# Layer 1's first-matmul weights of the first half: split ahead, kept in DRAM as fp16 pairs, read back in place

## The chip, the cores and the metric

The kernel runs on one core of a Trainium2 chip. The core has a matrix engine (TensorE, PE), a vector engine (VectorE, DVE), a scalar engine (ScalarE, ACT), a general engine (GpSimd, POOL) and a sync engine (SP), which here only issues DMAs; ACT and POOL issue DMAs too. Each engine works through its own list of instructions in order and waits on semaphores for the others. 16 DMA engines move data between DRAM (HBM) and the on-chip memory SBUF (128 partitions). The metric is the device time of one execution in microseconds (us), the median of several runs.

## What is computed

A gated scan over 10112 tokens of 256 numbers (two sequences of 5056), and after it two mixture-of-experts layers with 8 experts, each token going to one expert. Cut to what matters:

```
h = f[:, t] * h + (1 - f[:, t]) * x[:, t];  y[:, t] = h          # scan, f from f_logit and lower_bound
# layer 0 and layer 1 (other routers, the same shape)
expert_idx = argmax(logits, axis=1);  gate_w = max of softmax(logits)
for e in range(8):
    mask = expert_idx == e
    out[mask] = gate_w[mask, None] * (relu(x[mask] @ w1[e]) @ w2[e])   # w1[e] 256x1024, w2[e] 1024x256
```

All inputs and outputs are float32. The kernel keeps precision with fp16 pairs: a number times 64 is written as hi (rounded to fp16) plus lo (the remainder, fp16), and products of hi and lo parts are added up.

## The kernel before, in words

Tokens are sorted by expert into tables in DRAM (X[0] for layer 0, X[1] for layer 1), in tiles of 128 rows of one expert each. The hidden width of 1024 is cut into two halves of 512, h = 0 and h = 1. One **unit** is one tile with one half: `mm1` multiplies the transposed tile xT with the half's W1 (24 matmuls into a PSUM tile hps, line L801), `evac` makes the fp16 pair hT from it (ACT writes hi, L809, DVE writes lo), and three units later `mm2` multiplies hT with the half's W2 (L821, L824, into ops).

A host loop over **slots** writes the order of the whole program: slot i holds `mm1` and `evac` of unit i, `mm2` of unit i - 3 (`LAG`), and everything that `at(slot, priority, function, ...)` has put there, by priority. On PE, ACT, POOL and SP this written order is the order in which the engine works from slot 17 on; DVE's order is set by the framework's scheduler. There are 332 units: 166 of layer 0, then 166 of layer 1.

The weights of one half, all 8 experts, fill W1[h] and W2[h] in SBUF, and there is room for two halves. So around the change of layer the order of units is different (the **swap**): the last 21 tiles of layer 0 go through half 0 first (units 124 to 144) and then through half 1 (units 145 to 165). Once unit 144 is done, W1[0] and W2[0] are free, and during units 145 to 165 layer 1's half 0 is put there. Layer 1 begins with 21 tiles of half 0 (units 166 to 186), during which layer 1's half 1 is put in place.

A weight of one expert and half comes as 128 x 1024 float32 (512 KB) and is put in place in steps written by `wstep`: `w_load` brings it to a buffer ws (three buffers; a DMA that ACT issues, L371); two steps later `w_hi` writes hi with ACT (L384); three steps later `w_lo` writes lo with DVE (a SCALAR_TENSOR_TENSOR; most of DVE's work is recorded under helper lines, L183 for this form). `wplan(items, start, step)` puts 16 such items (8 of W1, 8 of W2) into slots `start + k * step`. For layer 1's half 0 these are slots 148 on, 0.98 slots apart.

Beside this, SP issues one transposing DMA per tile that brings xT from the table X (L770, four buffers, so that the one for unit u waits until unit u - 4 has read its buffer), and in layer 0 a small DMA exr (L783). After a tile's second half its result goes through the routing of layer 1: a chain over ACT, DVE, PE (x2p L910, logits lp L928, ranks RK) and POOL, which scatters the finished row trow into X[1] (L988). At slot 121 an If on all engines covers the last tiles of layer 0. The scan and the routing of layer 0 run beside the first units and end around slot 105; `checkpoint` then makes the last table of tiles, and POOL writes padding rows (L676) behind the tokens of each expert.

DMAs of SP and ACT signal their end on eight semaphores, DMAHW0 to DMAHW7, in turn (DMASW for POOL's); a DMA that gets a semaphore waits until the DMA that had it before has landed.

Of the kernel before, what the change touches and what calls it, by code (L numbers as in the profile page):

```python
# [10 lines left out]
F16 = mybir.dt.float16  # L11
I32 = mybir.dt.int32
U32 = mybir.dt.uint32
ACTF = mybir.ActivationFunctionType
ALU = mybir.AluOpType
AX = mybir.AxisListType

P = 128
D = 256
E = 8  # L20
F = 1024
HF = 512
# [39 lines left out]
 'sc': (0, 26),  # L62
 'exg': 'SSS',
 'w1': (-8, 0.8),
 'w2': (0, 0.75),
 'w3': (0, 0.9),
 'wprio': 60,
 'p': {'load': (-2, 2),
# [54 lines left out]
def scan_moe_moe_kernel(ctx, tc, xf, emb, cst, tmp, w1a, w2a, w1b, w2b, out, seq, cfg=CFG):  # L123
# [11 lines left out]
    LAG = cfg["lag"]  # L135
# [26 lines left out]
    qp = Pool(ctx.enter_context(tc.tile_pool(name="qp", bufs=6)))  # L162
# [7 lines left out]
    dr = ctx.enter_context(tc.tile_pool(name="dr", bufs=1, space=bass.MemoryType.DRAM))  # L170
# [2 lines left out]
    pr = ctx.enter_context(tc.tile_pool(name="pr", bufs=1, space=bass.MemoryType.PSUM))  # L173

    X = [dr.tile([DUM + P, RW // 2], I32, name=f"X{m}") for m in range(2)]
    W1 = [wp.tile([P, E, 2, 2, HF], F16, name=f"W1_{h}") for h in range(2)]
    W2 = [wp.tile([P, E, 4, 2, D], F16, name=f"W2_{h}") for h in range(2)]

    V, A, G, T, SP = nc.vector, nc.scalar, nc.gpsimd, nc.tensor, nc.sync

    def stt(eng, out, in0, s, in1, op0, op1, **kw):
        assert eng is V
        return eng.scalar_tensor_tensor(out=out, in0=in0, scalar=s, in1=in1, op0=op0, op1=op1, **kw)  # L183
# [180 lines left out]
    def w_load(item):  # L364
        m, which, h, e = item
        k = 8 * which + e
        if (m, h) == (0, 0) and k < 8 + cfg["wal"]:
            t = W1[1][:, k % 8].rearrange("p k b f -> p (k b f)").bitcast(F32)
        else:
            t = st.tile([P, 1024], F32, name="ws", tag="ws")  # L370
        hwq().dma_start(out=t, in_=wsrc[m][which][:, h, e, :])  # L371
        return t
# [13 lines left out]
    def w_lo(item, t):  # L386
        src, hi, lo = w_parts(item, t)
        m, which, h, e = item
        k = cfg["wg"][2 * m + h]
        i = 8 * which + e  # L390
        on_g = k and (i * k) // 16 != ((i + 1) * k) // 16
        if on_g:
            ts(G, src, src, 64.0, None, ALU.mult)
            tt(G, lo, src, hi, ALU.subtract)
        else:
            stt(V, lo, src, 64.0, hi, ALU.mult, ALU.subtract)

    def w_sub(item, t):

# [619 lines left out]
    for m in range(2):  # L1019
# [14 lines left out]
        for part in (tl, tails[m]):  # L1034
            for j in range(0, len(part), CT):
                d = dict(t=part[j:j + CT], at=j)
# [25 lines left out]
    def at(s, prio, fn, *a):  # L1062
        seqn[0] += 1
        slots.setdefault(s, []).append((prio, seqn[0], fn, a))
# [10 lines left out]
    for c in range(NCH):  # L1075
        b = s0[c]
# [9 lines left out]
        if c % 2 or c == NCH - 1:  # L1086
            q = c // 2
# [3 lines left out]
            b, prio = s0[c] + PO["put"][0], PO["put"][1]  # L1091
# [14 lines left out]
    def wseq(m, h):  # L1106
        return [(m, 0, h, e) for e in range(E)] + [(m, 1, h, e) for e in range(E)]

    wdone = set()
    wbuf = {}  # L1110
# [26 lines left out]
    def wplan(items, start, step, ahead=0):  # L1137
        x = start

        def it(k):  # L1140
            return items[k] if 0 <= k < len(items) else None

        if ahead:
            for k in range(len(items)):
                at(max(first - 2, int(start + (k - ahead) * step)), cfg["wlp"], wstep, it(k), None, None, None)
        for k in range(len(items) + 4):
            at(int(x), cfg["wprio"], wstep, None if ahead else it(k), it(k - 2), it(k - 3), it(k - 4))
            x += step

    last_h0 = [i for i, u in enumerate(units) if u[0]["m"] == 0 and u[1] == 0][-1]  # L1150
# [1 line left out]
    at(last0 + cfg["t0at"][0], cfg["t0at"][1], lambda: last_tiles(0))  # L1152
    wplan(wseq(0, 0), first + 1, cfg["wstep0"], cfg["wa"])
    wplan(wseq(0, 1), *cfg["w1"])
    wplan(wseq(1, 0), last_h0 + 1 + LAG + cfg["w2"][0], cfg["w2"][1] * cfg["swap"] / 16.0)
    wplan(wseq(1, 1), n1 + LAG + cfg["w3"][0], cfg["w3"][1] * cfg["swap"] / 16.0)

    loaded = [0]
# [232 lines left out]
```

## Time and profile before

| | |
|---|---|
| median of 3 runs | 1102.36 us (1089.52, 1102.36, 1105.03) |
| the profiled execution | 1096.34 us, span from first to last instruction 1094.5 us |
| mean granted clock of TensorE | 0.968 of full speed |
| PE busy | 983.7 us, 90% of the span |
| DVE busy | 684.3 us, 63% |
| ACT busy | 522.0 us, 48% |
| POOL busy | 505.1 us, 46% |
| moved by DMA | 124.12 MB, 113 GB/s over the span |

Shares over the span are averages over stages with different limits: the scan with layer 0's beginning, layer 0, the swap, layer 1. They are read stage by stage, with the waits and the rows of each. L-numbers are lines of the kernel; a line can be that of a helper, so groups are told apart by the tiles that they write and read (`W<-ws` is the split of a weight). SPq and ACTq are DMA issues on those engines' queues.

### The profile page before, as it was taken

The page shows a single profiled execution, that of the slowest core. Times are in us where ns is not written, and L with a number is a line of the kernel's source. Part 1 is how long each engine was busy: PE and PEld are TensorE (multiplying, and loading weights), DVE is VectorE, ACT ScalarE, POOL GpSimd, SP SyncE. Part 2 cuts the span into 40 slices and gives each one's busy share as a digit, 9 for nine tenths or more (in the row PEclk, how much of TensorE's full clock was granted, in tenths as well). Part 3 has the DMA queues.
Part 4 walks back from the last instruction along what each step waited for, and adds up shares of the span by engine and source line. Part 5 has one row for each costly group of instructions (what it writes and reads, how often), then busy time and mean ns, then how long its engine had stood idle before and what let it go on. Part 6 is the DMA issues. An engine that isn't in the chain of part 4 may idle for free.

```text
span 1094.5 us, 33440 instructions
## 1 busy us (share of the span) xinstructions
PE 983.7 (90%) x11935; PEld 795.2 (73%) x11935; DVE 684.3 (63%) x2116; ACT 522.0 (48%) x1298; POOL 505.1 (46%) x1009
## 2 busy tenths in 40 slices
PE   2532889999999999989999789999999999999996
PEld 2322668888888888867877678788788788788885
DVE  7867777888788777744649988866333333333332
ACT  5645556565656655444337655633333333333332
POOL 4888576667666666722103676145222222222222
PEclk9965999999999999998999999999999999999999
DMA  9448935676577765332339749943222322222120
GB/s 366 183 147 246 189 89 113 114 147 135 123 138 134 139 121 106 99 60 51 66 73 209 174 107 221 215 99 94 52 53 50 50 54 52 48 50 44 45 53 26
DMA packets 191620, 124.12 MB, mean 113 GB/s; under 512 B 169329, under 2 KB 170110, under 8 KB 191456
## 3 DMA queue, kind: packets, MB, share of 16 engines
q1 hardware_dynamic: 167344, 48.97, 24.7%
q10 hardware_dynamic: 11488, 39.33, 13.8%
q0 software_dynamic: 12624, 33.62, 11.2%
q8 instruction: 104, 1.70, 0.7%
q14 instruction: 60, 0.49, 0.2%
HBM read 54.70 MB, written 34.66 MB: 82 GB/s over the span
## 4 chain that ended last, share of the span: by engine, by line
PE 43%; DVE 5%; DMA 3%; issue 1%; POOL 1%; ACT 0%; POOLq 0%; DVEq 0%; ACTq 0%
PE hps L801 21%; PE ops L821 14%; PE ops L824 7%; DMA X<-trow,tsl 2%; DVE W L183 2%; DMA ws<-w2b 1%; DVE hT L183 1%; DMA ws<-w1b 1%; DVE trow L183 1%; DVE osum L191 1%; DVE trow L187 0%; POOL X L988 0%; DVE tsc L188 0%; POOL ob L191 0%; DVE tse L188 0%
## 5 line engine op out<-in xcount | busy, mean ns | idle before, releaser
L801 PE MATMUL hps<-xT,W 128*128 128x128 f16 x7968 | 506.4, 220 | 12.9 <-DMA xT<-X 10.0
L801 PEld LDWEIGHTS <-W 128*128 x7968 | 476.2, 98 | 53.8 <-issue 10.4
L821 PE MATMUL ops<-W,hT 128*128 x1328 | 452.6, 381 | 15.6 <-DVE hT L183 7.4
L183 DVE SCALAR_TENSOR_TENSOR hT<-hps,hT 128x512 f16<-128x512 f32 x332 | 228.2, 687 | 238.5 <-ACT hT L809 238.3
L824 PE MATMUL ops<-W,hT 128*128 x1328 | 363.5, 274 | 0.0
L809 ACT ACTIVATE hT<-hps 128x512 f16<-128x512 f32 x332 | 198.0, 597 | 300.0 <-PE hps L801 288.9
L821 PEld LDWEIGHTS <-hT 128*128 128x128 f16 x1328 | 130.1, 98 | 130.9 <-DVE hT L183 7.7
L1008 POOL DMA_INDIRECT out<-osum,ti x83 | 81.1, 977 | 290.4 <-DVE osum L183 259.0
L824 PEld LDWEIGHTS <-hT 128*128 128x128 f16 x1328 | 130.2, 98 | 18.5 <-issue 6.0
L988 POOL DMA_INDIRECT X<-trow,tsl x83 | 89.0, 1073 | 56.0 <-DVE tsl L191 30.5
L665 POOL DMA_INDIRECT X<-row,sl x79 | 87.0, 1101 | 37.5 <-issue 29.5
L842 ACT ACTIVATE ob<-ops,exr 128x256 f32<-128x256 f32 x83 | 39.3, 474 | 60.2 <-PE ops L824 58.9
L384 ACT ACTIVATE W<-ws 128x1024 f16<-128x1024 f32 x51 | 54.1, 1060 | 24.1 <-DMA ws<-w2a 7.5
L183 DVE SCALAR_TENSOR_TENSOR W<-ws,W 128x1024 f16<-128x1024 f32 x50 | 60.8, 1216 | 6.1 <-ACT W L384 5.9
L183 DVE SCALAR_TENSOR_TENSOR osum<-ops,exr,ob 128x256 f32<-128x256 f32 x83 | 40.2, 484 | 35.0 <-ACT ob L842 33.1
L505 PE MATMUL yt<-cs,xf 128*128 128x136 f32 x252 | 40.3, 304 | 13.8 <-issue 7.9
L840 ACT ACTIVATE ob<-ops 128x256 f32<-128x256 f32 x83 | 31.4, 378 | 40.2 <-PE ops L824 32.1
L191 POOL TENSOR_TENSOR ob<-ob,acc 128x256 f32<-128x256 f32 x25 | 21.8, 873 | 58.9 <-ACT ob L840 58.8
L505 PEld LDWEIGHTS yt<-cs,xf 128*128 128x128 f32 x252 | 34.5, 204 | 15.8 <-issue 8.7
L867 ACT ACTIVATE trow<-osum 128x256 f16<-128x256 f32 x83 | 35.0, 421 | 22.5 <-DMA X<-trow,tsl 13.5
L188 POOL TENSOR_SCALAR xf<-xf,fa,fb 128x256 f32<-128x256 f32 (+1 forms) x64 | 37.4, 591 | 17.3 <-ACT xf L453 15.8
L191 DVE TENSOR_TENSOR osum<-ops,ob 128x256 f32<-128x256 f32 x83 | 34.4, 415 | 14.9 <-ACT ob L840 10.4
(155 smaller groups left out, 1043.5 us busy)
## 6 DMA issues: line engine op xcount, KB each, us to landing
xf<-xf ACTq DMA_DIRECT2D x28, 512.0 KB
ws<-w1b ACTq DMA_DIRECT2D x16, 512.0 KB
ws<-w2b ACTq DMA_DIRECT2D x16, 512.0 KB
W<-xf SPq DMA_DIRECT2D x8, 512.0 KB
W<-w1a SPq DMA_DIRECT2D x8, 512.0 KB
ws<-w2a ACTq DMA_DIRECT2D x8, 512.0 KB
xT<-X SPq DMA_TRANSPOSE x212
ws<-w1a ACTq DMA_DIRECT2D x6, 512.0 KB
```

The source lines that it names most:

```text
L183: return eng.scalar_tensor_tensor(out=out, in0=in0, scalar=s, in1=in1, op0=op0, op1=op1, **kw)
L191: return eng.tensor_tensor(out=out, in0=in0, in1=in1, op=op)
L384: A.activation(out=hi, in_=src, func=ACTF.Copy, scale=64.0)
L505: T.matmul(out=yt[:, k * (P + E):(k + 1) * (P + E)], lhsT=t[:, k, i * P:(i + 1) * P], rhs=ide[:, (1 - k) * E:(1 - k) * E + P + E], start=T ...
L665: x_write(0, G.indirect_dma_start(out=X[0], out_offset=IndirectOffsetOnAxis(ap=p["sl"][:, i, 0:1], axis=0), in_=p["row"][:, i, :].bitcast( ...
L801: T.matmul(out=hps[:, c, :], lhsT=w, rhs=xt[:, a, :], start=(n == 0), stop=(n == 5))
L809: A.activation(out=hh[:, 0], in_=hps, func=ACTF.Relu)
L821: T.matmul(out=o.rearrange("p a d -> p (a d)"), lhsT=hT[:, k, :], rhs=W2u[h][:, ds(at4[k], 4 * D)].bitcast(F16), start=(first and k == 0), ...
L824: T.matmul(out=o[:, 0, :], lhsT=hT[:, 4 + k, :], rhs=W2u[h][:, ds(at4[k], 2 * D)].bitcast(F16), start=False, stop=(last and k == 3))
L842: A.activation(out=b, in_=o[:, 1, :], func=ACTF.Copy, scale=scale)
L988: x_write(1, G.indirect_dma_start(out=X[1], out_offset=IndirectOffsetOnAxis(ap=sl[:, i, 0:1], axis=0), in_=d["row"][:, i].bitcast(I32), in ...
L1008: i = ins_of(G.indirect_dma_start(out=out, out_offset=IndirectOffsetOnAxis(ap=ti, axis=0), in_=r, in_offset=None, bounds_check=N - 1, oob_ ...
```

## The change

The W1 weights of layer 1's half 0 are no longer loaded and split in the swap. `w_ahead` does this in slots 100 to 125 (`last0` is 124): load into ws, hi with ACT and lo with DVE into a buffer wq of the pool qp, and a store of the pair (512 KB) by SP to a DRAM tile WD. At slot 146 `w_fetch` reads the eight pairs back from WD straight into W1[0], with eight DMAs of SP. The loads and splits of the eight W2 weights start two slots earlier, at slot 146, and stand 1.51 instead of 0.98 slots apart. The first half's 16 items of layer 0 and the second half of layer 1 are not touched.

```diff
- 'w2': (0, 0.75),
+ 'w2': (-2, 1.15),
+ 'pre1': (-24, 2.3),
...
+    WD = dr.tile([P, E, 2 * 2 * HF], F16, name="WD")
...
+    def w_ahead(load, split, lo, store):
+        if store is not None:
+            SP.dma_start(out=WD[:, store, :], in_=wbuf.pop(("q", store)).rearrange("p k b f -> p (k b f)"))
+        if lo is not None:
+            q = wbuf["q", lo]
+            stt(V, q[:, :, 1], wbuf.pop(("a", lo)).rearrange("p (k f) -> p k f", k=2), 64.0, q[:, :, 0], ALU.mult, ALU.subtract)
+        if split is not None:
+            q = wbuf["q", split] = qp.tile([P, 2, 2, HF], F16, name="wq", tag="q")
+            A.activation(out=q[:, :, 0], in_=wbuf["a", split].rearrange("p (k f) -> p k f", k=2), func=ACTF.Copy, scale=64.0)
+        if load is not None:
+            wbuf["a", load] = w_load((1, 0, 0, load))
+
+    def w_fetch(e):
+        SP.dma_start(out=W1[0][:, e].rearrange("p k b f -> p (k b f)"), in_=WD[:, e, :])
+        wdone.add((1, 0, 0, e))
...
-    wplan(wseq(1, 0), last_h0 + 1 + LAG + cfg["w2"][0], cfg["w2"][1] * cfg["swap"] / 16.0)
+    for k in range(E + 4):
+        at(int(last0 + cfg["pre1"][0] + k * cfg["pre1"][1]), cfg["wprio"], w_ahead,
+           *(k - d if 0 <= k - d < E else None for d in (0, 2, 3, 4)))
+    for e in range(E):
+        at(last_h0 + 2, 58, w_fetch, e)
+    wplan(wseq(1, 0)[E:], last_h0 + 1 + LAG + cfg["w2"][0], cfg["w2"][1] * cfg["swap"] / 16.0)
```

What stands where in the built programs: first SP at the beginning of the swap, from the transpose for unit 147 on (the line numbers of the changed program are 19 higher from there on, so L789 is L770). Before:

```order
L770 DMA_TRANSPOSE xT<-X_99 128x4x128 [waits DMAHW5_49,PE_49]
L770 ISA
L770 DMA_TRANSPOSE xT<-X_99 128x4x128 [waits DMAHW7_49,DMAHW4_49,PE_49]
L759 TENSOR_LOAD tab
L770 ISA
L770 DMA_TRANSPOSE xT<-X_99 128x4x128 [waits DMAHW1_49,PE_49]
L770 ISA
L770 DMA_TRANSPOSE xT<-X_99 128x4x128 [waits DMAHW6_49,DMAHW2_49,PE_49]
```

and in the changed program, from the transpose for unit 149 on (W_0_102 is W1[0]):

```order
L789 DMA_TRANSPOSE xT<-X_99 128x4x128 [waits DMAHW1_49,PE_49]
L414 DMA W_0_102<-WD 128x2048 [waits DMAHW6_49]
L414 DMA W_0_102<-WD 128x2048
L414 DMA W_0_102<-WD 128x2048 [waits DMAHW0_49]
L414 DMA W_0_102<-WD 128x2048
L414 DMA W_0_102<-WD 128x2048 [waits DMAHW3_49]
L414 DMA W_0_102<-WD 128x2048 [waits DMAHW4_49]
L414 DMA W_0_102<-WD 128x2048 [waits DMAHW5_49]
L414 DMA W_0_102<-WD 128x2048 [waits DMAHW6_49]
L789 ISA
L789 DMA_TRANSPOSE xT<-X_99 128x4x128 [waits DMAHW2_49,DMAHW0_49,PE_49]
```

The eight reads stand between the transposes for units 149 and 150. They take the semaphores 6, 7, 0, 1, 3, 4, 5 and 6, in this order; 2 goes to ACT's first W2 load between them, and the transpose for unit 150 waits for semaphore 0, which the third read has.

Second, ACT in the first slots of the weight loads. Before, from slot 148 on (hT of unit 148 stands first; W_0_101 is W1[0]):

```order
L809 ACTIVATE hT<-hps 128x512 [waits PE_49]
L371 DMA ws<-w1b 128x1024 [waits DMAHW1_49]
L371 DMA ws<-w1b 128x1024 [waits DMAHW2_49]
L840 ACTIVATE ob<-ops 128x256 [waits DVE_49,PE_49]
L809 ACTIVATE hT<-hps 128x512 [waits PE_49]
L384 ACTIVATE W_0_101<-ws 128x2x512 [waits DMAHW1_49]
L371 DMA ws<-w1b 128x1024 [waits DMAHW4_49]
L867 ACTIVATE trow,tss<-osum 128x256 [waits DMASW1_49,DMASW7_49,DMASW0_49,DVE_49]
L840 ACTIVATE ob<-ops 128x256 [waits PE_49,Activation_49]
L809 ACTIVATE hT<-hps 128x512 [waits PE_49]
L384 ACTIVATE W_0_101<-ws 128x2x512 [waits DMAHW2_49]
```

and in the changed program from hT of unit 147 on (L828 is L809, L387 is L384, L374 is L371, and W_0_104 is W2[0]):

```order
L828 ACTIVATE hT<-hps 128x512 [waits PE_49]
L374 DMA ws<-w2b 128x1024 [waits DMAHW7_49]
L850 ACTIVATE ob<-ops 128x256 [waits DVE_49,PE_49]
L828 ACTIVATE hT<-hps 128x512 [waits PE_49]
L859 ACTIVATE ob<-ops 128x256 [waits DVE_49,PE_49]
L828 ACTIVATE hT<-hps 128x512 [waits PE_49]
L387 ACTIVATE W_0_104<-ws 128x4x256 [waits DMAHW2_49]
L374 DMA ws<-w2b 128x1024 [waits DMAHW4_49]
L886 ACTIVATE trow,tss<-osum 128x256 [waits DMASW1_49,DMASW7_49,DMASW0_49,DVE_49]
L859 ACTIVATE ob<-ops 128x256 [waits PE_49,Activation_49]
L828 ACTIVATE hT<-hps 128x512 [waits PE_49]
```

The loads are now of W2 alone, begin in slot 146 (the first stands just ahead of these rows) and come in two slots of three; the third waits for semaphore 4, which the sixth read has.

## Rows read from the trace of the kernel before

**Rows 1.** The page's first line.

```profile
span 1094.5 us, 33440 instructions
```

**Rows 2.** Stages: from:to length, busy us (count) by engine, PEclk, DMA share, GB/s.

```profile
440.00:500.00 60.00, 54.29 (x696) 44.08 (x695) 32.27 (x136) 26.27 (x69) 25.49 (x43) 0.94 0.28 69
510.00:558.00 48.00, 48.00 (x612) 38.83 (x609) 28.26 (x96) 19.64 (x43) 7.42 (x13) 1.00 0.35 63
558.00:583.00 25.00, 24.78 (x294) 19.60 (x293) 13.65 (x25) 12.63 (x27) 4.19 (x7) 1.00 0.62 136
583.00:634.00 51.00, 42.54 (x563) 34.46 (x562) 48.84 (x140) 35.05 (x82) 27.66 (x47) 0.97 0.73 171
634.00:660.00 26.00, 23.21 (x329) 19.02 (x328) 22.12 (x92) 15.10 (x41) 17.72 (x33) 1.00 0.54 118
694.00:1080.00 386.00, 386.00 (x4684) 310.41 (x4682) 159.17 (x262) 132.42 (x239) 96.79 (x161) 1.00 0.29 62
```

**Rows 3.** PE's waits, 569 to 660: releaser, us in total, times, longest.

```profile
PE ops L821 <- DVE hT L183: 7.4, 5, 2.4
```

**Rows 4.** Groups on DVE, 583 to 634: count, busy us, mean ns, idle before.

```profile
L183 DVE SCALAR_TENSOR_TENSOR W<-ws,W 128x1024 f16<-128x1024 f32 x14 | 17.0, 1211 | 0.0
```

**Rows 5.** Groups on PE, 583 to 634, same columns.

```profile
L801 PE MATMUL hps<-xT,W 128*128 128x128 f16 x312 | 20.4, 224 | 0.0
```

**Rows 6.** PE in order of time: start us, us, first-layer matmuls of one unit.

```profile
561.32 1.50 PE L801 MATMUL hps<-xT,W 128*128 128x128 f16 x24
563.96 1.50 PE L801 MATMUL hps<-xT,W 128*128 128x128 f16 x24
...
569.24 1.50 PE L801 MATMUL hps<-xT,W 128*128 128x128 f16 x24
...
574.75 1.50 PE L801 MATMUL hps<-xT,W 128*128 128x128 f16 x24
...
630.92 1.50 PE L801 MATMUL hps<-xT,W 128*128 128x128 f16 x24
...
637.05 1.50 PE L801 MATMUL hps<-xT,W 128*128 128x128 f16 x24
```

**Rows 7.** PE in order of time, the unit at 627.

```profile
627.05 2.38 PE L801 MATMUL hps<-xT,W 128*128 128x128 f16 x24
```

**Rows 8.** SP's issues in order of time, the program's start.

```profile
0.74 0.88 SPq L446 DMA_DIRECT2D W<-xf  x2
1.67 2.15 SPq L371 DMA_DIRECT2D W<-w1a  x4
```

**Rows 9.** ACT in order of time, the start: first and sixth transfer's user.

```profile
4.52 0.63 ACT L453 ACTIVATE W<-W 128x512 f32<-128x512 f32 x1 [1.01 <-DMA W<-xf]
...
13.18 1.06 ACT L384 ACTIVATE W<-W 128x1024 f16<-128x1024 f32 x1 [0.30 <-DMA W<-w1a]
```

**Rows 10.** Stages, the program's start; columns as in rows 2.

```profile
4.00:34.00 30.00, 8.28 (x34) 7.58 (x35) 22.78 (x60) 15.94 (x37) 15.33 (x29) 1.00 1.02 402
```

**Rows 11.** SP's issues in order of time, two transposes.

```profile
465.73 1.21 SPq L770 DMA_TRANSPOSE xT<-X  x1
...
562.85 1.19 SPq L770 DMA_TRANSPOSE xT<-X  x1
```

**Rows 12.** ACT in order of time, its first loads of the swap.

```profile
570.78 0.84 ACTq L371 DMA_DIRECT2D ws<-w1b  x2
```

**Rows 13.** PE in order of time around the If of slot 121.

```profile
488.50 1.50 PE L801 MATMUL hps<-xT,W 128*128 128x128 f16 x24
493.90 1.01 PE L910 MATMUL x2p<-id,trow 128*128 128x128 f16 x8 [3.89 <-PEq L1245]
...
497.37 2.35 PE L801 MATMUL hps<-xT,W 128*128 128x128 f16 x24
499.55 0.38 PE L821 MATMUL ops<-W,hT 128*128 x1
```

**Rows 14.** DMA queues, 570 to 620: packets, MB, share of 16 engines (q10 is ACT's).

```profile
q10 hardware_dynamic: 2034, 7.41, 54.8%
```

**Rows 15.** PE in order of time, the wait for the last table's first tile.

```profile
468.83 1.39 PE L801 MATMUL hps<-xT,W 128*128 128x128 f16 x22 [1.82 <-DMA xT<-X]
```

## The prediction

> **What bounds the kernel now.** I read first the busy times by stage, then PE's waits, then the groups of one stretch, then single rows in order of time. In the long stage of layer 1 PE is busy 386.0 of 386 us, and from 510 to 558 it is busy 48 of 48 [rows 2]: there only PE's own work counts, and the change touches none of it. PE loses time in the swap, where layer 0's second half runs while layer 1's first-half weights are put into the freed tiles. A unit with nothing beside it takes 2.64 us (561.32 to 563.96), and one with the routing of its rows 3.065 us, half of the pair from 630.92 to 637.05 [rows 6]. From 583 to 634 PE does 312 first-layer matmuls, which is 13 units of 24 [rows 5]; at 3.065 us they need 39.8 us and take 51, so 11.2 us are lost. Who is late? PE waits 7.4 us in five waits for hT, which DVE writes [rows 3], and DVE is busy 48.84 of these 51 us [rows 2]. Of this, 17.0 us are 14 splits of weights at 1.21 us each [rows 4]. So DVE bounds this stretch, PE everything after it. The remainder of the 11.2 us is smaller waits and PE running at half its clock: the matmuls of the unit at 627.05 take 2.38 us where 1.50 is normal [rows 7], after a wait of 2 us.
>
> **What the change does, term by term.** Eight of the 16 splits leave the swap; slots 100 to 125 get them instead, with eight stores of 512 KB on SP's queue; and slot 146 gets eight reads of 512 KB on SP's queue. All of PE's rows stay as they are.
>
> Relief. DVE's work from 583 to 634 without splits is 48.84 - 17.0 = 31.8 us. After the change eight splits (W2 alone) are left. Their second steps stand at slots 146 + 1.51k with k from 3 to 10: 150, 152, 153, 155, 156, 158, 159 and 161. The stretch starts with slot 153, so two fall before it, where DVE has room (13.65 of 25 us busy from 558 to 583 [rows 2]), and six in it: 6 x 1.21 = 7.3 us. DVE then needs 39.1 us and PE 39.8. Before, DVE reached 48.84/51 = 96% of its stretch; at that share 39.1 us take 40.8, and the gain is 51 - 40.8 = 10.2 us. The bounds: 11.2 if PE never waits, and 5.7 if the loss lies in the length of the chain from PE over DVE, ACT and POOL and not in DVE's load. The latter is read from 634 to 660, where almost no split is left and PE still stands 2.8 of 26 us idle [rows 2]; that share of 51 us is 5.5, and 11.2 - 5.5 = 5.7. I take 10.2. ACT is spared its eight first steps too, beside DVE's work, which counts nothing more.
>
> The reads back. SP runs one transpose per unit with four buffers, so the transpose for unit 149 is issued when unit 145 has been read, at 562.85, and takes SP 1.19 us [rows 11]. In the changed order the eight reads stand right behind it, ahead of the transpose for unit 150. When does that one have to be there? ACT's first weight loads of slot 148 start at 570.78 [rows 12], behind the unit that starts at 569.24; two units later, at 574.75, unit 150 starts [rows 6]. When would it land? The nearest rows are the program's start, where SP issues transfers of the same size back to back from 0.74 us [rows 8]. ACT's waits for them end in the order of issue: the first at 4.52, the sixth at 13.18 [rows 9], which is 1.73 us each; the eighth would land 0.74 + 3.78 + 7 x 1.73 = 16.6, or 15.9 us after the first issue. By bytes: 4.19 MB at the 402 GB/s of that stretch [rows 10] take 10.4 us, two loads of ACT in the same time (1.05 MB) 2.6, and 2.5 us pass before the first bytes are counted (first transfer 3.78 us after its issue, less 1.3 for its bytes), together 15.5. From 564.1 the last read lands at 579.6. A transpose undisturbed is used 3.1 us after its issue starts, 1.9 us after it ends (465.73 to 468.83 [rows 11, 15]); behind the reads I add 1.0 for its own bytes. Unit 150 starts at 580.6 instead of 574.75: a stall of 5.8 us. Later transposes queue right behind and PE needs one only every 2.64 us or more, so it happens once. Bounds: nothing, if a transpose does not queue behind the reads (beside ACT's weight loads no wait for xT shows among PE's waits from 569 to 660); and 12.2 us, if the reads move at the rate of ACT's loads from 570 to 620, 7.41 MB in 54.8% of 50 us, 270 GB/s [rows 14]: 15.5 for the reads, 3.9 for the two loads and 2.5 before them, so 564.1 + 21.9 + 1.0 = 587.0. I take 5.8, since queue, size and back-to-back issue are those of the start.
>
> [...]
>
> The built program adds a wait on top. Eight semaphores serve the DMAs of SP and ACT in turn, so the transpose of unit 150 is not issued before the third read has landed (some 7 us after the first issue, 571, by the 1.73 us each; then 1.2 of issue), and ACT's third W2 load, behind its first split, not before the sixth (about 577). Both lie ahead of 579.6. Behind ACT's load stand the output copies and hT of unit 150, which PE itself starts at 580.6, so it costs nothing while the stall lasts.
>
> [...]
>
> The early half. From 440 to 500 ACT is busy 26.3 of 60 us, DVE 32.3, the DMA engines 28% [rows 2]; eight splits (9.7 us of DVE's, a little less of ACT's) and 8.4 MB of loads and stores fit. One place is tight: the first transposes of layer 0's last table wait for the padding rows that POOL writes, and PE waited 1.8 us for them [rows 15]. A split ahead of POOL's indices or a store's bytes can add up to one split, 1.2 us; at best nothing. I take 1.0. The first two stores stand ahead of that transpose in SP's order, but SP idles there until 465.73.
>
> Sum: -10.2 + 5.8 + 2.8 + 1.0 = -0.6 us. The profiled execution took 1096.3 us (span 1094.5 [rows 1]), so 1095.7. It lies 6.1 us below the median of the runs, 1102.4; the mean of all four times is 1098.3, 2.0 above it. I forecast 1095.7 + 2 = 1097.7 us.
>
> **The rivals** (each with the same 2 us added).
> B, the reads are hidden: the transpose lands in time, no stall and no clock loss. 1096.3 - 10.2 + 1.0 + 2 = 1089. For it: transposes beside ACT's loads never held PE up. Against: those loads were in another queue and came one or two a unit, not eight at once.
> C, slower: the reads share the DMA engines with transposes, loads and scatters and move at 270 GB/s; PE stands 12.2 us and loses 2.8 by the clock. 1096.3 - 10.2 + 15.0 + 1.0 + 2 = 1104. It decides from the point where the stall passes 10.2 - 2.8 - 1.0 = 6.4 us, that is when the last read lands after 580.15; the start's rows give 579.6, which is close.
> D, the relief does not come: with fewer splits the chain of routing steps still takes its time, as from 634 to 660. 1096.3 - 5.7 + 5.8 + 2.8 + 1.0 + 2 = 1102.
>
> **Chances.** The forecast 0.42 (its own range 1093 to 1101), B 0.27, C 0.17, D 0.14. The range reaches from B, some 4 us lower for a fast set of runs, to C with 5 us more, since the median of these runs lies 4 us above the mean I used: 1085 to 1109. A measurement of this kernel tells some 2% from no change, 22 us; all four cases lie inside that, so within 2% is 0.94. Faster by over 2% needs under 1080, B with perfect relief and a low set of runs: 0.03. Slower by over 2%, over 1124, needs C and a second stall as long: 0.03.
>
> **What would show it.** In the profile after: DVE with six splits in 13 units and about 41 us for them; one wait of PE for xT of some 6 us two units after the loads of W2 begin, with half the clock for a few us behind it; SP's reads issued from about 564 us on; the wait for xT at 469 not over 3 us; layer 1's stage unchanged at 2.64 us a unit. I am wrong if that one wait is missing or over 10 us, if PE waits for hT beside the early splits, or if the 13 units still take over 46 us.

## The result, and the profile after

The changed kernel took 1103.13 us (median of 20 runs; the kernel before 1094.37 beside it), a ratio of 1.0084 with a 95% interval of 1.006 to 1.0107: 9 us slower, by less than 2%. The time lies in the forecast's range, 5 us above its 1097.7 and next to rival C's 1104, but not by C's mechanism. That it comes so close is in part luck: the forecast's base, 1098.3, was 4 us above what the kernel before took beside the changed one, and as a change the forecast was -0.6 us. In one set of the runs below (first two splits on ACT, reads in ACT's queue, splits from unit 125 on) every kernel, the one before too, took some 32 us longer, so each ratio is to the kernel before of the same set. The profiled execution took 1104.0 us; the page's first line answers to [rows 1]:

```profile
span 1101.9 us, 33479 instructions
```

So this trace is 7.4 us longer than that of before. To find where, I went through PE's rows in order of time in both traces and took the start of each unit's first-layer matmuls, numbered as the prediction numbers slots and units. The excess of units a to b is the time between these two starts, less the same time in the kernel before. From unit 20 to 113, from 115 to 121, from 123 to 149 and from 186 to the end it is 0.1 us or less. The rest:

```
units      excess us   what
4-20         +1.8      start of the program; nothing is changed there, and the other
                       profiles (the kernel before again, too) have -4.8 to +0.8
113-115      +7.1      wait for the transpose of unit 114, then half clock
121-123      -0.6      the If of slot 121
149-151      +8.4      wait for the transpose of unit 150, then half clock
153-166      -8.6      the 13 units of the swap: 51.2 us before, 42.6 after
166-186      -0.9      end of the swap
sum          +7.2      (7.4 by the spans)
```

The relief and the stall of the reads are there as forecast. The third large number, +7.1 at unit 114, is the one that the forecast had at +1.0.

The stages answer to [rows 2] (from:to length, busy us and count of PE, PEld, DVE, ACT and POOL, PEclk, DMA share, GB/s; the swap lies later by some 8 us, then by 17):

```profile
440.00:500.00 60.00, 52.50 (x679) 42.60 (x675) 40.48 (x151) 32.69 (x74) 29.27 (x46) 0.94 0.68 184
583.00:593.00 10.00, 3.09 (x27) 2.76 (x26) 2.02 (x3) 1.40 (x5) 0.72 (x1) 0.66 1.07 282
593.00:634.00 41.00, 40.00 (x540) 32.61 (x539) 38.59 (x118) 28.61 (x74) 23.74 (x42) 1.00 0.49 119
694.00:1080.00 386.00, 385.66 (x4673) 310.07 (x4673) 163.22 (x269) 135.82 (x245) 96.90 (x161) 1.00 0.31 66
```

In the stretch of the swap PE is now busy 40 of 41 us, where it was 42.5 of 51. The price stands in the row above it: 10 us in which PE works 3.1. PE's waits from 569 to 660 (releaser, us in total, times, longest) no longer name hT of [rows 3]; the second row below is the remainder of DVE's chain. DVE's splits in 41 us are seven instead of the 14 of [rows 4] (busy us, mean ns, idle before):

```profile
PE hps L820 <- DMA xT<-X: 6.9, 1, 6.9
PE RK L450 <- DVE ter L194: 3.3, 4, 1.3
```

```profile
L186 DVE SCALAR_TENSOR_TENSOR W<-ws,W 128x1024 f16<-128x1024 f32 x7 | 8.5, 1218 | 0.3 <-ACT W L387 0.3
```

The two lost places in PE's order of time (start us, us, the wait ahead of the row in brackets). Before, the first of them waited 1.82 us [rows 15] and the second not at all [rows 6]. The 24 matmuls take 2.72 us instead of 1.50:

```profile
475.50 2.72 PE L820 MATMUL hps<-xT,W 128*128 128x128 f16 x24 [6.54 <-DMA xT<-X]
```

```profile
590.22 2.72 PE L820 MATMUL hps<-xT,W 128*128 128x128 f16 x24 [6.91 <-DMA xT<-X]
```

In both places the granted clock was half, 0.50 (columns as in rows 2):

```profile
475.50:478.00 2.50, 2.50 (x24) 2.49 (x24) 0.00 (x0) 0.00 (x0) 0.45 (x1) 0.50 0.81 185
590.20:592.90 2.70, 2.68 (x25) 2.66 (x25) 0.00 (x0) 0.00 (x0) 0.00 (x0) 0.50 0.68 221
```

SP's issues that belong to them, in order of time: the transpose of unit 114, the eight reads, the transpose of unit 150.

```profile
471.70 1.21 SPq L789 DMA_TRANSPOSE xT<-X  x1
```

```profile
572.49 4.06 SPq L414 DMA_DIRECT2D W<-WD  x8
```

```profile
579.91 1.20 SPq L789 DMA_TRANSPOSE xT<-X  x1
```

The transpose of unit 150 is issued only at 579.91, 3.4 us after the last read (it waits for the third read's semaphore; SP's longest wait for a read there is 3.2 us), and is used 10.3 us after its issue; undisturbed that took 3.1 [rows 11, 15].

For unit 114 one has to look at POOL. Its transpose needs the padding rows of layer 0's last table, which POOL scatters after other scatters, in order. Four of POOL's scatter issues, each 0.97 to 1.0 us before, took longer, and each of the four began while DVE made one of the splits ahead. First POOL's four, then DVE's four:

```profile
443.31 1.67 POOL L684 DMA_INDIRECT X<-row,sl  x1 [0.31 <-DVE tsl L194]
...
451.84 1.90 POOL L695 DMA_INDIRECT X<-zrow,pads  x1 [0.30 <-issue]
...
459.34 1.29 POOL L1007 DMA_INDIRECT X<-trow,tsl  x1 [0.30 <-issue]
...
463.50 1.81 POOL L1007 DMA_INDIRECT X<-trow,tsl  x1 [0.30 <-DVE tm L964]
```

```profile
442.90 1.23 DVE L186 SCALAR_TENSOR_TENSOR wq<-ws,wq 128x1024 f16<-128x1024 f32 x1
...
451.67 1.23 DVE L186 SCALAR_TENSOR_TENSOR wq<-ws,wq 128x1024 f16<-128x1024 f32 x1 [0.26 <-ACT ob L859]
...
458.56 1.23 DVE L186 SCALAR_TENSOR_TENSOR wq<-ws,wq 128x1024 f16<-128x1024 f32 x1 [0.82 <-ACT wq L409]
...
463.23 1.23 DVE L186 SCALAR_TENSOR_TENSOR wq<-ws,wq 128x1024 f16<-128x1024 f32 x1
```

Add start and length in both: the splits end at 444.13, 452.90, 459.79 and 464.46, the scatters at 444.98, 453.74, 460.63 and 465.31, each 0.84 or 0.85 us later. That looks as if POOL could not go on before the split was over. The trace of the kernel before shows the same in the swap, where the splits stood until now: this split ends at 608.64, and the scatter that begins inside it at 609.48, 0.84 us later.

```profile
607.43 1.21 DVE L183 SCALAR_TENSOR_TENSOR W<-ws,W 128x1024 f16<-128x1024 f32 x1
```

```profile
607.66 1.82 POOL L988 DMA_INDIRECT X<-trow,tsl  x1 [0.30 <-issue]
```

### The profile page after: what moved, and what is told of

It reads as the page before. It is cut to its first block, busy times and chain, and to the rows that moved or that the text cites. A ratio compares the mean times of both kernels' runs of the same rounds, so it can differ in the third digit from the quotient of the medians.

```text
span 1101.9 us, 33479 instructions
## 1 busy us (share of the span) xinstructions
PE 985.1 (89%) x11935; PEld 796.8 (72%) x11935; DVE 683.6 (62%) x2116; ACT 522.2 (47%) x1298; POOL 506.0 (46%) x1009
## 4 chain that ended last, share of the span: by engine, by line
PE 43%; DVE 4%; DMA 2%; issue 2%; POOL 2%; ACT 0%; ACTq 0%; POOLq 0%; DVEq 0%
PE hps L820 22%; PE ops L840 14%; PE ops L843 7%; DVE W L186 1%; DMA X<-trow,tsl 1%; DMA xT<-X 1%; DVE hT L186 1%; POOL X L1007 1%; POOL ob L194 1%; DVE trow L186 0%; DVE trow L190 0%; DVE acc L194 0%; DVE osum L194 0%; DVE pi L191 0%; POOL inv L191 0%
## 5 line engine op out<-in xcount | busy, mean ns | idle before, releaser
L828 ACT ACTIVATE hT<-hps 128x512 f16<-128x512 f32 x332 | 198.1, 597 | 306.5 <-PE hps L820 294.5
L186 DVE SCALAR_TENSOR_TENSOR W<-ws,W 128x1024 f16<-128x1024 f32 x42 | 51.1, 1217 | 3.9 <-ACT W L387 3.7
L387 ACT ACTIVATE W<-ws 128x1024 f16<-128x1024 f32 x43 | 45.5, 1057 | 15.4 <-DMA ws<-w2a 8.7
```

Of the source, the lines that this page charges most:

```text
L387: A.activation(out=hi, in_=src, func=ACTF.Copy, scale=64.0)
L828: A.activation(out=hh[:, 0], in_=hps, func=ACTF.Relu)
```

## The experiments

My theory was that the three large numbers of the table belong to three parts that can be taken apart: the relief, the block of reads, and the place of the splits ahead. Its rival was that one of them hides in another, above all that the relief is smaller when nothing delays the swap.

### The relief alone

```diff
-    for k in range(E + 4):  ... w_ahead ...
-        at(last_h0 + 2, 58, w_fetch, e)
+        wdone.add((1, 0, 0, e))
```

> Changed kernel without the early loads, splits and stores and without the reads back (layer 1's first-half W1 is then never brought in, so layer 1 multiplies with layer 0's): only the relief of the swap is left. My theory: the 13 units from 153 to 165 get 8 us shorter and the units to 185 another 1.5, so about 9.5 us under the kernel before, ratio 0.991; PE waits for xT as in the kernel before (1.8 us at unit 114, none at unit 150). Rival (the chain of routing steps, not DVE's load, sets the swap): no more than 6 us under before, ratio 0.995.

Measured: 1083.95 us against 1093.88, ratio 0.9913 (0.988 to 0.9946). Units 113 to 115 and 149 to 151 have an excess of 0.0, units 153 to 166 one of -8.5. What the change takes away is worth 9.5 us of the kernel (5.9 to 13.1 by the interval).

### The reads spread, the splits later, and both

```diff
-        at(last_h0 + 2, 58, w_fetch, e)
+        at(last_h0 + 2 + 2 * e, 58, w_fetch, e)
```

> Changed kernel with the eight reads back in slots 146, 148, ... 160 instead of all in slot 146; the early part stays. My theory (4 MB in one go stand ahead of one transpose): the wait of 6.9 us at unit 150 and the half clock behind it go, 8 us faster than the changed kernel, ratio to before 1.001. Rival (the bytes themselves cost): the wait is split into several of 1 us each at units 150 to 164, together as long, ratio near 1.008.

Measured: 1096.13, ratio 1.0029 (1.0 to 1.0057). The stall at unit 150 is gone (excess 0.0), the wait at 114 stays (+6.2). The rival is not quite out: the relief of units 153 to 166 is only -2.4 us in this profile, with waits behind DVE and one of 1.1 us for a transpose. In the other four profiles with spread reads it is -7.1 to -8.3, against -8.4 to -8.9 where the reads are in one block on SP's queue or left out. So spreading is not free: it costs 6 us of the relief here and up to 1.5 there, where the splits ahead stand elsewhere too. Besides, units 182 to 186 lost 6.5 us here in waits behind late loads of W2 for layer 1's second half; it came back in some profiles (+5.4 and +4.7 in two runs below) and not in others, and I have no cause for it.

```diff
- 'pre1': (-24, 2.3),
+ 'pre1': (-11, 2.1),
```

> Changed kernel with the early part moved from slots 100 on to slots 113 on, so that no split and no store stands ahead of the padding rows and of the last table's first transpose; the reads back stay. My theory (the early part costs 7 us at unit 114 because of what it puts ahead of that transpose): PE's wait at unit 114 goes back from 6.5 to about 2 us, the half clock behind it goes, and the kernel is 7 us faster than the changed one, 2 us over before (ratio 1.002). Rival (8.4 MB more of DMA cost the same wherever they stand): the wait moves to a later unit and the ratio stays near 1.008.

Measured: 1097.45, ratio 1.0048 (1.002 to 1.0077). The stall at 150 is there (+9.5). At 114 the excess is 3.2, not 0: the first load now goes out at 465.57, beside the transpose, which is issued in time (465.30, 465.73 before) but used 4.99 us later instead of 3.1. So bytes beside the transpose are enough to delay it.

Both edits at once:

> The early part from slot 113 on and the reads in slots 146, 148, ... 160. My theory: both stalls go and the relief stays, 9.5 us less 1 to 2 of contention: 8 us under the kernel before, ratio 0.993. Rival (contention moves elsewhere): not under 0.998.

Measured: 1091.93, ratio 0.9988 (0.9961 to 1.0016), less of a gain than expected. The 3.0 us at unit 114 are those of the run before.

### Who delays unit 114?

Two theories stood against each other: the splits on DVE hold POOL back (V), or the loads and stores slow scatters and transpose (W). The first try gave the second halves of the first two splits to ACT:

```diff
+            if lo < 2:
+                A.activation(out=q[:, :, 1], in_=..., func=ACTF.Copy, scale=64.0)
+            else:
                 stt(V, q[:, :, 1], ...)
```

> The changed kernel, but the second halves of the first two splits ahead are written by ACT (a plain copy, the remainder is left out for two of eight experts, so the output is less exact); DVE has then no split ahead of the routing results that POOL waits for, while loads, stores and the other six splits stand as they were. Theory V (the two splits of 1.23 us on DVE hold back POOL's indices, and the transposes behind its padding rows): the transpose for unit 114 is issued within 1.5 us of its time before (465.7 by the start of unit 113 and not 4 us late), PE's wait there is 2 to 3.5 us instead of 6.5, the excess of units 113 to 115 falls from 7.1 to 0.5 to 2.5 us, and the whole kernel is at 1.002 to 1.005. Theory W (loads and stores on the DMA engines slow POOL's scatters and the transpose, whatever DVE does): the wait stays at 5 to 6.5 us, the excess at 5 to 7 us, the kernel at 1.007 to 1.009.

Measured: 1129.46 against 1126.24, ratio 1.0033 (1.0012 to 1.0054), which would be V. But in this kernel and two more below (splits from unit 125 on, reads in ACT's queue) PE waited for "issue" in places that no edit touches, unit 113 among them, so I don't count the excess of 5.9 there. Another run, undisturbed, with all eight second halves on ACT:

> The changed kernel, but the second halves of all eight splits ahead are written by ACT as a plain copy (the remainder is left out, so the output is less exact); loads, stores and reads stand as they were. In the changed kernel five scatter issues of POOL lasted 1.3 to 1.9 us instead of 0.97, and each of them ended 0.84 to 0.94 us after the end of one of DVE's splits. Theory V (DVE's splits, which keep POOL from writing its scatters while they run and stand in DVE's order ahead of the routing, are the cause): no scatter issue from units 106 to 114 over 1.2 us, the transpose for unit 114 issued 2 to 3 us after unit 113 starts (2.0 before, 6.0 in the changed kernel), PE's wait there 1.8 to 3 us, excess of units 113 to 115 from 0 to 2, whole kernel 1.002 to 1.005. Theory W (loads and stores on the DMA engines): long scatters stay, transpose 4 to 6 us after unit 113 starts, excess 5 to 7 us, kernel 1.007 to 1.010.

Measured: 1102.48 against 1094.65, ratio 1.0083 (1.0049 to 1.0117). V is refuted as the whole cause. No scatter from unit 106 on is stretched any more, and the last one ends 2.5 us sooner after the start of unit 113 than in the changed kernel; still the excess is 6.8. Last scatter, transpose and unit 114:

```profile
466.44 1.04 POOL L695 DMA_INDIRECT X<-zrow,pads  x1 [0.30 <-issue]
```

```profile
471.00 1.21 SPq L789 DMA_TRANSPOSE xT<-X  x1
```

```profile
476.41 1.87 PE L820 MATMUL hps<-xT,W 128*128 128x128 f16 x16 [6.76 <-DMA xT<-X]
```

From the scatter's end to the transpose's issue 3.5 us (1.95 before), from there to PE 5.4 (3.1 before): the time has moved from POOL to the transfers. This run does not isolate the transfers, though: ACT makes eight steps more in it, and its last scatter still ends 1.1 us later than before. With the next pair the two are taken apart. The kernel before ran once more beside this run:

> The kernel before once more, for its profile in the same session as the next three: in the last session its runs took 1126 us and in the earlier ones 1094, and the kernels profiled there show PE waiting for 'issue' about units 106 to 113 and 180 to 182. If that lies in the session and not in the edits, the kernel before shows it too when its runs are slow, and shows none (span 1085 to 1100) when they are fast.

Measured: 1090.59 us (one execution), span 1088.8, no "issue" wait from 160 us on, excess 0.0 at units 113 to 151. The rows of before are repeatable there. Outside those three profiles such waits come to 0.5 us at most from 160 us on, in them to 19 to 22.

Transfers alone (loads on ACT's queue, stores on SP's, two steps earlier than in the changed kernel, no split, no read):

```diff
     def w_ahead(load, split, lo, store):
         if store is not None:
-            SP.dma_start(out=WD[:, store, :], in_=wbuf.pop(("q", store))...)
-        if lo is not None: ...
-        if split is not None: ...
+            SP.dma_start(out=WD[:, store, :], in_=wbuf.pop(("a", store)))
```

> The relief alone with the transfers of the splits ahead and nothing else of them: eight loads of 512 KB on ACT's queue in the changed kernel's slots (100 to 116), each stored again unchanged to DRAM on SP's queue two steps behind its load; no split of ACT or DVE, no reads back (layer 1 multiplies with layer 0's first-half W1, so the output is not the reference's). The excess of units 113 to 115 was 7.1 us in the changed kernel and 6.8 with the splits taken off DVE. If the transfers alone do it (theory W), it is 5 to 7 here, with the transpose for unit 114 used 4.5 to 6 us after its issue. If it takes the splits on DVE and ACT (theory V), 0 to 2.5. If each adds its part to a chain that PE already waits for (theory X), 2.5 to 5, and this number and that of the next run add up to 7 within 2 us, the half clock behind a longer wait counted once. POOL's scatter issues stay at 0.97 to 1.1 us in every case. Whole kernel: 0.991 of the relief plus this.

Engine work alone (both steps of each split on a constant in SBUF, no load, store or read):

> The relief alone with the engine work of the splits ahead and nothing else of them: ACT's first steps and DVE's two-input second steps of 128x1024 in the changed kernel's slots, reading a constant in SBUF; no load, no store, no reads back (layer 1 multiplies with layer 0's first-half W1, so the output is not the reference's). Theory V: the excess of units 113 to 115 is 5 to 7 us, three to five scatter issues of POOL between units 106 and 114 last 1.2 to 1.9 us and end 0.8 to 0.95 us behind the end of a split; the transpose for unit 114 is issued 4.5 to 6 us after unit 113 starts (2.0 before). Theory W: 0 to 1.5 us, transpose at 2 to 2.5. Theory X: 2.5 to 5.

Measured: transfers alone 1090.18 against 1095.42, ratio 0.9963 (0.9919 to 1.0007), excess at 114 of 4.0; engine work alone 1090.20, ratio 0.996 (0.9921 to 0.9999), excess 3.8. Each is close to the relief's 0.9913 plus its 4 us. Theory X holds in its number: each adds its part. Unit 114 starts 2.6 us late by the transfers and 2.1 by the engine work, together the changed kernel's 4.7; the half clock behind it (the unit's 24 matmuls take 2.72 us in each) costs 1.3, 1.6 and 2.4. The transfers' transpose and PE:

```profile
462.42 1.21 SPq L783 DMA_TRANSPOSE xT<-X  x1
```

```profile
466.06 1.22 PE L814 MATMUL hps<-xT,W 128*128 128x128 f16 x10 [4.44 <-DMA xT<-X]
```

The engine work's: a scatter held by a split, both with no transfer of weights anywhere, and PE. (The name in PE's wait is that of an instruction long done; the transpose was issued at 467.93 and is what came last, 3.07 us later.)

```profile
441.04 1.23 DVE L186 SCALAR_TENSOR_TENSOR wq<-cs,wq 128x1024 f16<-128x1024 f32 x1
```

```profile
441.45 1.66 POOL L682 DMA_INDIRECT X<-row,sl  x1 [0.30 <-DVE tsl L194]
```

```profile
471.00 1.23 PE L818 MATMUL hps<-xT,W 128*128 128x128 f16 x10 [3.96 <-DVE wq L186]
```

Worked out in the same way for all: how much later than before, counted from the start of unit 113, the last scatter of padding rows ends; what is added from there to the transpose's issue and from there to PE; and what unit 114 itself takes more, at half clock.

```
us more than before      scatters   landing   transpose   half clock   sum
changed kernel             3.56       0.46       0.70         2.36     7.1
none on DVE                1.06       1.57       2.31         1.88     6.8
transfers alone            0.02       2.06       0.54         1.34     4.0
engine work alone          2.37      -0.20      -0.03         1.63     3.8
one input, engines alone   0.77      -0.21       0.07         1.65     2.3
```

Part by part the two do not add up to the first line: 2.4 us of scatters against 3.6, 1.9 of landing against 0.5. That their sums meet is shown, not that each link costs the same in company.

The last line is a run that was to tell whether it is the split's two operands in SBUF that hold POOL. It replaced DVE's step by a multiply with one operand:

> As the run before, but DVE's second step reads one operand of SBUF instead of two (a multiply by a constant; same size, same place). If the scatter issues of POOL are held because a split reads two operands of SBUF, all of them from units 106 to 114 last 0.97 to 1.1 us here, while DVE is as busy as before if the instruction takes 1.1 to 1.2 us; if it is any long DVE instruction, those that overlap one still last 1.2 to 1.9 us. If the instruction runs in half the time, about 0.55 to 0.6 us, and the scatters still stretch by some 0.3 us, that is the second case.

Measured: 1084.87 us (one execution), excess 2.3. The instruction took 0.68 us, and no scatter lasted over 1.2. It doesn't separate the two, though: of the scatters beside a split one had begun 0.05 us ahead of it (0.97 us, not held), and of two that began inside one, the later (at 456.19, the split ending at 456.39) ended at 457.24, again 0.85 us behind the split. The other lasted 1.07 us, as in the kernel before. Which property of the instruction holds POOL stays open; that a shorter one costs less is shown.

### What holds the transpose of unit 150?

Either the eight reads ahead of it in SP's queue (Q), or the DMA engines that are full (S). One word is changed, the queue:

```diff
-        SP.dma_start(out=W1[0][:, e]..., in_=WD[:, e, :])
+        A.dma_start(out=W1[0][:, e]..., in_=WD[:, e, :])
```

> The changed kernel with one thing altered: the eight reads of slot 146 are issued by ACT instead of SP; number, place and bytes are the same. In the changed kernel the transpose for unit 150 was issued 3.4 us late (behind the third read's semaphore) and was used 10.3 us after its issue, 3.1 being normal; PE waited 6.9 us. Theory Q (the transpose is behind the reads in SP's own queue): with the reads in ACT's queue the transpose goes round them; use 3 to 5 us after issue, PE's wait at unit 150 under 2.5 us, excess of units 149 to 151 under 3 us, whole kernel 1.000 to 1.003. Theory S (the 16 DMA engines are simply full for 12 us, whoever issues): use 8 to 10 us after issue, wait for xT at unit 150 still 5 to 7 us and the excess 7 to 9, whole kernel 1.006 to 1.010. Either way ACT is held some 4 us by issuing, which may show as a wait for hT of up to 3 us about unit 147.

Measured: 1126.85 against 1126.24, ratio 1.0012 (0.9987 to 1.0036). PE doesn't wait for the transpose of unit 150 any more, and units 149 to 151 lose 2.7 us: as theory Q had it. But PE waits 2.46 us for the next transpose, which neither theory had, and the excess of units 149 to 153 is 4.3 us instead of 8.4. The single rows don't tell why; the packets by queue and stretch tell more (q1 is SP's queue, q10 ACT's). A transpose is some 550 packets of under 512 B, 0.13 MB (546 from 587.5 to 590 in this run, where nothing else moved); a read's packets are of some 4 KB (102 of them and 9 small ones carry 0.42 MB in the changed kernel's microsecond from 586). In the changed kernel, from 574 to 587, while the reads' 4 MB move in SP's queue, and then from 587.5 to 590.2:

```profile
DMA packets 1382, 5.09 MB, mean 391 GB/s; under 512 B 143, under 2 KB 143, under 8 KB 1381
```

```profile
DMA packets 1346, 0.42 MB, mean 156 GB/s; under 512 B 1322, under 2 KB 1322, under 8 KB 1346
```

Hardly a small packet moves in 13 us, and then 1322 in 2.7 us. In the first six of the 13 no transpose was in the queue, since that of unit 150 was issued only at 579.91; from then on the transposes stood behind all the reads. With the reads in ACT's queue, from 592 to 597, and then from 599.4 to 604.6 (packets, MB, share of 16 engines):

```profile
q10 hardware_dynamic: 484, 1.79, 92.4%
q1 hardware_dynamic: 550, 0.13, 12.2%
```

```profile
q10 hardware_dynamic: 395, 1.45, 90.2%
q1 hardware_dynamic: 396, 0.09, 10.6%
```

Here the transpose of unit 150, issued at 590.10, gets through early: of the 550 packets of SP's queue in the first stretch 509 move in two single microseconds, from 593 and from 595, beside 161 of ACT's, and 41 in the other three, beside 323. The transpose of unit 151, issued at 592.74, doesn't. From 597 on about one small packet moves for each large one, of the reads and of the loads of W2 behind them (247 beside 256 up to 599.4, then 396 beside 395), and PE gets this tile only 11.9 us after the issue:

```profile
599.40 1.50 PE L820 MATMUL hps<-xT,W 128*128 128x128 f16 x24
...
604.67 1.62 PE L820 MATMUL hps<-xT,W 128*128 128x128 f16 x20 [2.46 <-DMA xT<-X]
```

So Q is the cause of the long wait at unit 150, and half of the loss comes back one unit later, in the sharing of the DMA engines that S meant. Nor are reads free in ACT's queue: issuing them takes ACT 6.5 us, its first split of W2 waits 6.4 us for a load behind them, and the relief shrinks to -4.7. In one queue, then, 1322 small packets moved behind the reads' 4 MB; between two queues 396 moved beside 395, but 509 beside 161 as well, and no run here shows what sets this share.

### A place where the splits cost nothing

First between unit 125 and 143, where PE had never waited, with the reads spread:

```diff
- 'pre1': (-24, 2.3),
+ 'pre1': (1, 1.7),
```

> The changed kernel with both of its costs taken away: the splits ahead are put into slots 125 to 143 (first load behind the last transposes that wait for padding rows and behind the If of slot 121; from 510 to 558 us PE never waits before), and the eight reads back are spread, one every second slot from 146. My theory (what costs is only where each piece stands: +7.1 us at unit 114 by the splits ahead, +8.4 at unit 150 by the reads in one block, and the relief of about 8.5 to 9.5 us is unharmed): no excess at units 113 to 115 and 149 to 151, 8 us less in units 153 to 186, some 0.5 to 1 us more in units 125 to 145, so 0.9925 (0.990 to 0.995). Rival (16 MB more of traffic and eight splits cost the same wherever they stand, since DVE and the DMA engines have no room in layer 0's second half): 3 to 6 us come back as waits for hT or xT in units 125 to 145, and the ratio is 0.996 to 1.001, as it was with the splits in slots 113 to 136.

Measured: 1121.86 against 1126.24, ratio 0.9959 (0.9933 to 0.9986). The gain is half of the relief. In units 123 to 149 there are 4.3 us more, in waits that the stretch didn't have, as the rival said (though its 16 MB more of traffic are 8.4: 132.5 MB against 124.1). Of them 3.2 us are waits behind DVE or behind ACT's hT, and 0.5 is one of the "issue" waits (PE's waits from 520 to 600):

```profile
PE ops L840 <- DVE acc L194: 1.2, 1, 1.2
PE ops L840 <- ACT hT L828: 1.1, 2, 0.9
PE hps L820 <- DVE wq L186: 0.9, 1, 0.9
```

Then with the first load behind the transposes that need padding rows, and a wider step:

```diff
+ 'pre1': (-7, 2.2),
```

> The changed kernel with the splits ahead in slots 117 to 141 at 2.2 slots each (first load behind the transposes that wait for layer 0's last padding rows) and the reads spread as before, one every second slot from 146. If the 3.0 us that were left at unit 114 with the start in slot 113 came from the first load's 512 KB beside the transpose for unit 114, the excess of units 113 to 115 is now 0 to 0.5 us; relief -8 us in units 153 to 186; in units 123 to 149, where the denser plan (1.7 slots) lost 4.3 us behind DVE's splits, 1.5 to 4 us. Sum -4 to -6.5, ratio 0.994 to 0.9965. Rival (the work ahead costs some 3 to 4 us wherever it stands, by splits that PE's chain over DVE meets): excess 3 to 5 us in units 117 to 149 and 0.9965 to 0.999.

Measured: 1086.45 against 1094.65, ratio 0.9923 (0.988 to 0.9967). This kernel leaves nothing out and is faster than both: excess -0.1 at units 113 to 115, 0.0 from 123 to 151, -7.6 from 153 to 166, and the +4.7 at units 182 to 186 that come and go. PE's only wait for a transpose from 440 to 660 is the old one of [rows 15]:

```profile
PE hps L820 <- DMA xT<-X: 1.7, 1, 1.7
```

The same with each DVE split in two halves, one step apart:

> As the run before, but each of DVE's splits ahead is made in two halves of 0.6 us, one slot-step apart, so that no routing step or accumulation of DVE stands behind 1.23 us at once (ACT's first half comes one step sooner in turn). If what PE loses in units 123 to 149 is the length of one DVE instruction in its chain (three waits of 0.9 to 1.2 us with the whole splits), the excess there falls to 0 to 1.5 us and the ratio to 0.992 to 0.995; if it is DVE's total load or the traffic, it stays at 2 to 4 us and the ratio at that of the run before, within 0.001.

Measured: 1087.20, ratio 0.9945 (0.9916 to 0.9974). There was nothing left to gain in units 123 to 149 (0.0 with whole splits at this step, 1.5 with halves), so the question of the halves fell away; the denser plan was what had cost the 4.3 us, not the length of one instruction by itself. That plan also began eight slots later, and the step and the start were not tried apart.

## Why the prediction came out wrong, step by step

Against its own time the sum gave 1095.7, and the profiled execution took 1104.0, 8.3 us more: 6.1 from the early half, 0.8 from the relief, -0.2 from the stall with its clock, and 1.8 from the program's start and -0.6 from the If of slot 121, which the change doesn't touch. The remaining 0.4 is spread.

**Relief: right.** Forecast -10.2, with 5.7 and 11.2 as ends; measured -9.4 over units 153 to 186 in the changed kernel, and in the run with the relief alone -7.7 over the same units and 9.5 us (5.9 to 13.1) of the whole kernel. The 13 units took 42.6 us, not 40.8, but the units behind them gave 0.9 more. That the steps of the weights and not the chain's length set this stretch is shown, and rival D is out. That it was DVE's share of these steps is argued from PE's waits: the change takes eight steps from ACT as well, and no run parts the two.

**Reads: right in mechanism and sum.** One stall, at the transpose two units after W2's loads begin, of 6.9 us (forecast 5.8), and 1.3 at half clock behind it (forecast 2.8): 8.4 by unit starts against 8.6. No run shows the sum's 2.8 us for the clock; what the runs showed in its place is this 1.3, and 1.3 to 2.4 at unit 114. That the transpose stands behind the reads in SP's queue no row of before showed; the packets do (143 small ones in 13 us, then 1322 in 2.7), and the run with the reads in ACT's queue halves the loss (4.3 us). Rival B's missing stall came with the reads one by one (excess 0.0 at units 149 to 151); C's slow reads did not come: 391 GB/s in all while they moved, not 270.

**Splits ahead: the step that failed.** The prediction saw the right place ("One place is tight") and read the right row, PE's wait of 1.8 us for the padding rows [rows 15]. It failed at "A split ahead of POOL's indices or a store's bytes can add up to one split, 1.2 us". The sign it had named for this place, a wait of not over 3 us, came out at 6.5. It should have read that wait as the end of a chain without slack: PE already stands there, so all that any link loses goes straight into the time. Then it should have counted what the links meet: four splits, not one, by the time of this transpose; POOL held by them (3.56 us later, of which 2.8 are four stretched scatters); loads and stores beside the scatters' landing and the transpose (1.2 us; loads and stores were not tried apart); and half clock behind a longer wait (2.4 us), which it had priced for unit 150 and not here. Busy shares of 26 and 32 of 60 us [rows 2], on which "fit" rested, say nothing about that. The price of a held scatter could have been read ahead: the swap of the kernel before has a scatter of 1.82 us behind a split, where 0.97 is normal. The runs of transfers alone (+4.0) and engine work alone (+3.8) show that either half of the work would have passed the bound of 1.2.

**Sign.** With 1.0 at this place the change was within a microsecond of nothing. The balance was 9.4 of gain against 8.4 of a known price, and the one term taken lightly decided it. The kernel in which both prices are avoided by place alone, at 0.9923, shows that the change itself was sound.

## What to carry to other kernels

Where the engine that bounds the kernel already waits for a chain, however briefly, work put beside links of this chain is paid in time: here 4.0 us for the transfers alone and 3.8 for the engine work alone, of which 1.3 and 1.6 are slow clock behind the longer wait; look for such waits before placing work by busy shares, and start the new work behind the last of them. Put bulk reads one by one between small transfers of the same queue, not in a block ahead of one that is needed soon; here that saved the 8.4 us, at a price of up to 1.5 us of the relief in four profiles of five, and of 6 in the fifth. Let work in an idle-looking stage come sparsely: at 2.2 slots a step it was free here; at 1.7, and from a later slot on, it cost 4.3 us.

## What the runs showed of the hardware

A scatter that POOL begins while DVE makes a split of 128x1024 with two operands in SBUF is finished 0.84 or 0.85 us after the split's end: four of four in the changed kernel up to unit 114, three more in the run of engine work alone, with no transfer of weights at all. Later ones in the same traces are finished up to 0.94 us after it. One that began within 0.03 us of a split's start was not held (0.98 us, in the run of engine work alone), and that split took 1.29 instead of 1.23. The other way round nothing was held, in the changed kernel: a scatter of 1.07 us was under way from 457.96 when the split of 458.56 began, and this took its 1.23 us. By what a split holds the scatters, and through which operand, none of my runs shows.

How long PE waits and what the clock then costs did not go together. Behind 1.82 us (before) unit 114 took its normal 2.64 us; behind 2.45 us, in the run with the one-operand step, it lost 1.65 us (its 24 matmuls took 2.62 us); behind 6.54 us, in the changed kernel, 2.36 at a granted clock of 0.50; behind 6.91 us, at unit 150, only 1.33 at the same 0.50. Why it is so no run here shows.
